# RetNet attention and a soft mixture of experts on one Trainium2 core: the remainder's steps and batch 1's steps in another order, the start's casts and the down weights' layout changed

## The chip, the cores and the metric

The kernel runs on one core of one Trainium2 chip. The metric is the device time of one execution in microseconds. Three runs of the kernel before gave 570.39, 568.17 and 568.40 us; the median is 568.4. One execution was profiled, and every instruction time below comes from it.

## The reference

Two stages, the second on the first one's output. Sizes: batch B = 8, heads H = 8, sequence S = 576, head width D = 64; N = 4608 tokens, model width 512, E = 4 experts, F = 1024.

```python
gamma = 1.0 - 2.0 ** (-5.0 - np.arange(H))
Dmat = np.where(rel >= 0, gamma[:, None, None] ** rel, 0.0)     # rel = i - j
ret = (q @ k.T / sqrt(D)) * Dmat                                # no softmax
x = (ret @ v) as [B * S, H * D]
p = domain_probs / (domain_probs.sum(-1, keepdims=True) + 1e-09)
for e in range(E):
    h = np.maximum(x @ w1[e], 0.0)
    out += p[:, e:e + 1] * (h @ w2[e])
```

Every token passes through all four experts.

## The kernel before, in words

**Attention in chunks.** The decay splits into a factor per query and one per key. Keys are multiplied with theirs when they are cast to bf16 (`cast`, tables `gk`), results with the query's when they leave PSUM (`gq`). What stays is a lower triangle, so the 576 positions of a batch are worked as four chunks of 128 and a remainder of 64 (R). Within a chunk: scores (keys by queries) times a triangle `tri`, then values. From the chunks before: a state, keys transposed by values, summed over the chunks in PSUM (`kvp`) and copied by ScalarE after each chunk to `sbd`, two heads as a block diagonal. Heads go in four pairs (NP = 4).

The methods, with the lines of the profile:

- `cast` (L222, L224; L375 to L379 for batch 0) and `cast_rem` (L227, L230): float32 to bf16, on the engine given.
- `Tc`, `Trem` (L285, L249): transposes of queries and keys by TensorE; `dmaT` (L256): the same by DMA, issued by SP.
- `S` with `Smat` and `Smask` (L264, L271): scores of two head pairs over all chunks, then the masks on VectorE. `Sc` (L297, L301): scores of one chunk for all pairs. `Srem` (L324, L328): scores of the remainder.
- `O` (L338 values, L343 states, L347 product on VectorE into `xT`), `Oc` (L310, L315, L317) and `Orem` (L354, L359, L361): results of two pairs, of one chunk, of the remainder.
- `kv` (L237, L242): state of one chunk.

Batch 0 has a class of its own, `AttP`, which works in four units (two halves of the sequence by two halves of the heads; L389 to L457) as its inputs land. Batch 1 is worked chunk by chunk (`Tc`, `Sc`, `kv`, `Oc`), batches 2 to 7 by head pairs. PSUM has three buffers for the experts (`ps_mm`), four for attention (`ps_at`, in turn) and one for states.

**Experts in tiles of 512 tokens.** `moe(nt)` is a generator for one of nine tiles. For each expert it makes eight blocks of `hT` (four 512-wide matmuls each, `ph`, L468; ScalarE's Relu copies them out, L487), then four blocks of output (eight 512-wide matmuls each, `po`, L497), which ScalarE writes (first expert, L501) or VectorE adds to `acc` (L503). After each block it yields, so a tile has 48 groups. Matrices are named by their tiles: up `wt_267`, `wt_496`, `wt_500`, `wt_504` for experts 0 to 3, down `wt_491`, `wt_498`, `wt_502`, `wt_506`.

**What sets the order.** Every engine works through its own queue in program order, and the program is written out by hand: `plan` maps a group's number to the attention steps put behind that group. TensorE meets the attention of batch nt + 1 between the matmuls of tile nt. For batches 2 to 7:

```python
            at(19 if nt == 1 else 17, lambda: state["A"].S([0, 1]))
            at(24, lambda: state["A"].O([0, 1]))
            at(27, lambda: state["A"].S([2, 3]))
            at(32, lambda: state["A"].O([2, 3]))
            at(37, lambda: state["A"].Srem())
            at(40, lambda: state["A"].Orem())
```

Batch 1 goes into groups 40 to 47 of tile 0: `Tc(c)` at 40, 42, 44, 46, `Sc(c)` and `kv(c)` one group later, `Oc(c)` another group later. The last chunk's scores and results stand between the tiles, around the first three half blocks of tile 1 (`lead`).

**The start.** SP issues the loads of batch 0 in twelve parts (L85). GpSimd casts keys and values of each unit and, for the second unit, queries; ScalarE casts the other units' queries (L377). GpSimd also issues the loads of weights, which convert float32 to bf16 on the way: the first up matrix in two halves (L119), behind key casts of the third and fourth unit, then the first down matrix (`load_w2`, L124) and the other six. The first matmul of the experts is at 19.43 us.

A down matrix is loaded with two neighbouring rows for each partition; row pairs mean that hidden unit 2p + i of a block of 256 stands in partition p, so `up` takes every second column of the up matrix (L467).

Of the kernel before, what the change touches and what calls it, by code (L numbers as in the profile page):

```python
# [9 lines left out]
FP32 = mybir.dt.float32  # L10
# [4 lines left out]
MULT = mybir.AluOpType.mult  # L15
# [5 lines left out]
def kernel(  # L21
# [10 lines left out]
    nc = tc.nc  # L32
    B, H, S, D = q.shape
# [6 lines left out]
    R = S - NCH * C  # L40
    SM = NCH * C
    NP = H // 2
# [7 lines left out]
    allp = list(range(NP))  # L50
# [9 lines left out]
    ps_at = ctx.enter_context(tc.tile_pool(name="ps_at", bufs=4, space=PSUM))  # L60
# [12 lines left out]
    state = {}  # L73
# [39 lines left out]
    w1_sb, w2_sb = [], []  # L113
# [7 lines left out]
    def load_w2(e):  # L121
        wt2 = wpool.tile([128, NFC, Dm], BF16, tag=f"w2_{e}", name="wt2")
        w2_sb.append(wt2)
        return nc.gpsimd.dma_start(out=wt2[:, :, :].rearrange("p (fo fi) d -> p fo (fi d)", fi=2),  # L124
                                   in_=moe_w2[e].rearrange("(fo p fi) d -> p fo (fi d)", p=128, fi=2))


    load_paired(0)
# [49 lines left out]
    gq = const.tile([128, NP, S], FP32)  # L178
# [7 lines left out]
    sbd = const.tile([128, NCH, NP, 128], BF16)  # L186
# [15 lines left out]
    xT = const.tile([128, NDC, N], BF16)  # L202
# [5 lines left out]
    class Att:  # L208
# [120 lines left out]
                    st[:, j], s[j], tri[:R, :R].unsqueeze(1).to_broadcast([R, NP, R]), op=MULT)  # L329
            self.sT["r"] = st  # L330

        def O(self, pairs):
            b = self.b
            os = [ps_at.tile([128, SM], FP32, tag="at", name="o") for _ in pairs]
            for p, o in zip(pairs, os):
                for c in range(NCH):
                    for j in range(2):
                        nc.tensor.matmul(o[64 * j:64 * j + 64, c * C:(c + 1) * C],  # L338
                                         lhsT=self.m["v"][:, c, 2 * p + j, :], rhs=self.sT[p][:, j, c, :],
                                         start=(c == 0), stop=False, skip_group_check=True)  # L340
            for p, o in zip(pairs, os):
                for c in range(1, NCH):
                    nc.tensor.matmul(o[:, c * C:(c + 1) * C], lhsT=sbd[:, c - 1, p, :],  # L343
                                     rhs=self.qkT[:, 0, p, c * C:(c + 1) * C],
                                     start=False, stop=(c == NCH - 1), skip_group_check=True)
            for p, o in zip(pairs, os):
                nc.vector.tensor_tensor(xT[:, p, b * S:b * S + SM], o, gq[:, p, 0:SM], op=MULT)  # L347

        def Orem(self):
            b = self.b  # L350
            o = ps_at.tile([128, NP, R], FP32, tag="at", name="orem")
            for p in range(NP):
                for j in range(2):
                    nc.tensor.matmul(o[64 * j:64 * j + 64, p, :],  # L354
                                     lhsT=self.r["v"][:, 2 * p + j, :], rhs=self.sT["r"][:, j, p, :],
                                     start=(p == 0), stop=False, skip_group_check=True)
            for n in self.rem_states:
                for p in range(NP):
                    nc.tensor.matmul(o[:, p, :], lhsT=sbd[:, n, p, :], rhs=self.qkT[:, 0, p, SM:S],  # L359
                                     start=False, stop=(p == NP - 1), skip_group_check=True)  # L360
            nc.vector.tensor_tensor(xT[:, :, b * S + SM:(b + 1) * S], o, gq[:, :, SM:S], op=MULT)  # L361

# [96 lines left out]
    def moe(nt, lead=0):  # L461
        n0 = nt * NT

        def up(ph, e, fc, ts):
            for dc in range(NDC):

                w = w1_sb[e][:, dc, (fc // 2) * 256:(fc // 2 + 1) * 256].rearrange("p (f i) -> p f i", i=2)  # L467
                nc.tensor.matmul(ph[:, ts], lhsT=w[:, :, fc % 2],  # L468
                                 rhs=xT[:, dc, n0 + ts.start:n0 + ts.stop], start=(dc == 0), stop=(dc == NDC - 1))

        acc = [apool.tile([128, Dm], FP32, tag="acc", name="acc") for _ in range(NSUB)]
        for e in range(E):
            hT = hpool.tile([128, NFC, NT], BF16, tag="hT")
            for fc in range(NFC):
                if e == 0 and fc < lead:
                    if fc == 0:
                        early = [ps_mm.tile([128, NT], FP32, tag="mm", name="ph") for _ in range(lead)]
                        for x in range(lead):
                            up(early[x], e, x, slice(0, NT // 2))
                            if x != 1:  # L480
                                yield
                    ph = early[fc]
                    up(ph, e, fc, slice(NT // 2, NT))
                else:
                    ph = ps_mm.tile([128, NT], FP32, tag="mm", name="ph")
                    up(ph, e, fc, slice(0, NT))
                nc.scalar.activation(hT[:, fc, :], ph, Relu)  # L487
                yield
            for ns in range(NSUB):
                t = nt * NSUB + ns  # L490
                pe = probs[:, e, t:t + 1]
                last = t == NTT - 1 and e == E - 1
                w = Dm // 2 if last else Dm
                for d in range(0, Dm, w):
                    po = ps_mm.tile([128, w], FP32, tag="mm", name="po")
                    for fc in range(NFC):
                        nc.tensor.matmul(po, lhsT=hT[:, fc, ns * 128:(ns + 1) * 128],  # L497
                                         rhs=w2_sb[e][:, fc, d:d + w], start=(fc == 0), stop=(fc == NFC - 1))
                    a = acc[ns][:, d:d + w]
                    if e == 0:  # L500
                        nc.scalar.activation(a, po, Copy, scale=pe)  # L501
                    else:
                        nc.vector.scalar_tensor_tensor(a, po, pe, a, op0=MULT, op1=ADD)  # L503
                    if e == E - 1:
                        eng = nc.scalar if last and d // w % 2 else nc.sync
                        eng.dma_start(out=out[n0 + ns * 128:n0 + (ns + 1) * 128, d:d + w], in_=a)
                yield


    a0 = AttP(0)  # L510
# [7 lines left out]
    for x, (hf, u) in enumerate(UNITS):  # L518
        a0.T(hf, u, nc.scalar)
        if x < 2:  # L520
            load_gq((2 + x,))
        if x == 0:
            warm(4)
        else:
            a0.O(*UNITS[x - 1])
        if x < 3:
            a0.cast("k", *UNITS[x + 1], nc.gpsimd)
            if x:
                load_w1(0, x - 1)
            a0.cast("q", *UNITS[x + 1], nc.scalar if x else nc.gpsimd)  # L530
            a0.cast("v", *UNITS[x + 1], nc.gpsimd)
        a0.S(hf, u)
        if x == 0:
            warm(2)
        a0.kv(hf, u)
# [14 lines left out]
    for nt in range(n_nt):  # L550
        plan = {}

        def at(g, *fs):
            plan.setdefault(g, []).extend(fs)

        if nt == 0:
# [17 lines left out]
            for c, g in enumerate((40, 42, 44, 46)):  # L574
                at(g, lambda c=c: state["a1"].Tc(c))
                if c < 3:
                    at(g + 1, lambda c=c: state["a1"].Sc(c), lambda c=c: state["a1"].kv(c, allp))
                    at(g + 2, lambda c=c: state["a1"].Oc(c))
            at(47, lambda: state["a1"].kv(3, allp))
        elif nt + 1 < B:  # L580
            if nt == 1:
                a1 = state["a1"]
                at(0, lambda: a1.cast_rem(nc.gpsimd))
                at(2, a1.Trem)
                at(4, a1.Srem)
                at(6, a1.Orem)
            def begin(b=nt + 1):
                A = state["A"] = Att(b)
                for c in range(NCH):
                    for n in "kqv":  # L590
                        A.cast(n, c, nc.gpsimd)
                A.cast_rem(nc.gpsimd)
                for c in range(NCH + 1):
                    A.dmaT(c)
                if b + 1 < B:
                    load(b + 1)

            at(7 if nt == 1 else 0, begin)
            for n, g in zip(range(NCH), (13, 15, 17, 18) if nt == 1 else (9, 11, 13, 15)):
                at(g, lambda n=n: state["A"].kv(n, allp))  # L600
            at(19 if nt == 1 else 17, lambda: state["A"].S([0, 1]))
            at(24, lambda: state["A"].O([0, 1]))
            at(27, lambda: state["A"].S([2, 3]))
            at(32, lambda: state["A"].O([2, 3]))
            at(37, lambda: state["A"].Srem())
            at(40, lambda: state["A"].Orem())
        for g, _ in enumerate(tiles[nt]):
            for f in plan.get(g, ()):
                f()
# [35 lines left out]
```

## Time and profile before

| what | value |
|---|---|
| three runs | 570.39, 568.17, 568.40 us; median 568.4 |
| the profiled execution | 570.39 us |
| its span, first to last instruction | 568.6 us, 8301 instructions |
| TensorE matmuls busy | 555.3 us, 98% |
| TensorE weight loads busy | 264.9 us, 47% |
| VectorE, ScalarE, GpSimd busy | 159.1, 228.9, 95.1 us |
| mean granted clock of TensorE | 0.993 |
| one steady tile, from one expert block to the same one of the next tile (213.28 to 273.58 us) | 60.3 us |

Matmuls are pipelined, and each is listed with its whole length, so the starts tell more than the busy time: a 512-wide matmul is listed with 379 ns, but 32 of them start within 6.91 us. "PEld" is TensorE's weight load; "64*128" in a matmul's row are the rows and columns of the array that it uses, and "64x128 bf16" its moving operand. A timeline row gives start, length, engine, line, operation, tiles and how many instructions it merges.

### The profile page before, as it was taken

Reading aid. Unit: us, or ns where it says so; the run is one execution under the profiler, and the core shown is the slowest. Engines: PE = TensorE matmul, PEld = TensorE weight load, DVE = VectorE, ACT = ScalarE, POOL = GpSimd, SP = SyncE. Lnnn points to the kernel's source line nnn. Section 1 sums busy time; section 2 is a strip of 40 time slices with the busy share of each in tenths; the row PEclk is TensorE's granted clock in tenths of the full one; section 3 lists DMA queues with packets and bytes.
Section 4 is the critical chain, followed back from the end, with each engine's and each line's share of the span. In section 5 each row is a group of like instructions: output and inputs, shape, how many; then the busy total and the mean of one; then the engine's idle time right before and its main releaser. Section 6 shows DMA issues by size and latency. Waiting matters only on the chain.

```text
span 568.6 us, 8301 instructions
## 1 busy us (share of the span) xinstructions
PE 555.3 (98%) x3418; PEld 264.9 (47%) x3418; DVE 159.1 (28%) x267; ACT 228.9 (40%) x409; POOL 95.1 (17%) x141
## 2 busy tenths in 40 slices
PE   7699999999999999999999999999999999999997
PEld 4444455444444444444444444444444444444443
DVE  5203254054204420342124320542044202220222
ACT  6252354622363235533463236223632353335332
POOL 7400437015001420114010601050000000000000
PEclk9799999999999999999999999999999999999999
DMA  9999997493259015940577037802300100010002
GB/s 234 202 206 205 207 196 175 84 206 46 83 93 221 11 39 115 194 63 1 134 159 115 1 111 140 159 1 84 74 2 1 50 25 1 0 66 10 1 0 75
DMA packets 146102, 53.84 MB, mean 95 GB/s; under 512 B 130540, under 2 KB 137964, under 8 KB 146064
## 3 DMA queue, kind: packets, MB, share of 16 engines
q1 hardware_dynamic: 141168, 44.79, 37.8%
q0 software_dynamic: 4752, 8.39, 8.0%
q8 instruction: 27, 0.44, 0.3%
q10 hardware_dynamic: 144, 0.13, 0.1%
q14 instruction: 11, 0.09, 0.1%
HBM read 45.16 MB, written 9.44 MB: 96 GB/s over the span
## 4 chain that ended last, share of the span: by engine, by line
PE 95%; DMA 2%; SPq 1%; DVE 0%; issue 0%; ACT 0%; POOL 0%
PE ph L468 44%; PE po L497 44%; DMA wt_267<-in_moe_w_dram 1%; PE o L338 1%; PE kvp L237 1%; SPq L85 1%; DMA raw_k<-in_k_dram 1%; PE o L343 1%; PE orem L354 0%; PE orem L359 0%; PE ptc L285 0%; PE oc L310 0%; PE oc L315 0%; POOL km L375 0%; ACT sbd L242 0%
## 5 line engine op out<-in xcount | busy, mean ns | idle before, releaser
L487 ACT ACTIVATE hT<-ph 128x512 bf16<-128x512 f32 x288 | 171.7, 597 | 279.3 <-PE ph L468 277.8
L497 PEld LDWEIGHTS <-hT 128*128 128x128 bf16 x1160 | 112.5, 98 | 131.4
L503 DVE SCALAR_TENSOR_TENSOR acc<-po,probs,acc 128x512 f32<-128x512 f32 (+1 forms) x109 | 81.3, 746 | 225.9 <-PE po L497 219.0
L468 PE MATMUL ph<-xT,wt_267 128*128 128x512 bf16 (+1 forms) x312 | 66.9, 372 | 5.5 <-DMA wt_267<-in_moe_w_dram 4.7
L468 PE MATMUL ph<-xT,wt_496 128*128 128x512 bf16 x288 | 66.8, 379 | 0.0
L468 PE MATMUL ph<-xT,wt_504 128*128 128x512 bf16 x288 | 66.2, 379 | 0.0
L468 PE MATMUL ph<-xT,wt_500 128*128 128x512 bf16 x288 | 65.8, 379 | 0.0
L497 PE MATMUL po<-wt_502,hT 128*128 128x512 bf16 x288 | 64.6, 379 | 0.0
L497 PE MATMUL po<-wt_491,hT 128*128 128x512 bf16 x288 | 64.4, 379 | 0.0
L497 PE MATMUL po<-wt_506,hT 128*128 128x512 bf16 (+1 forms) x296 | 64.1, 373 | 0.0
L497 PE MATMUL po<-wt_498,hT 128*128 128x512 bf16 x288 | 64.0, 379 | 0.0
L222 POOL TENSOR_TENSOR km<-raw_k,gk 128x512 bf16<-128x512 f32 x28 | 29.2, 1042 | 148.2 <-PE kvp L237 81.8
L468 PEld LDWEIGHTS <-wt_267 128*128 128x128 bf16 x312 | 30.9, 101 | 37.6 <-DMA wt_267<-in_moe_w_dram 5.1
L468 PEld LDWEIGHTS <-wt_500 128*128 128x128 bf16 x288 | 27.4, 98 | 31.5
L468 PEld LDWEIGHTS <-wt_504 128*128 128x128 bf16 x288 | 27.2, 98 | 30.7
L468 PEld LDWEIGHTS <-wt_496 128*128 128x128 bf16 x288 | 27.0, 98 | 28.8
L501 ACT ACTIVATE acc<-po,probs 128x512 f32<-128x512 f32 x36 | 24.7, 687 | 36.1 <-PE po L497 36.1
L224 POOL CAST vm<-raw_v 128x512 bf16<-128x512 f32 x28 | 17.2, 614 | 96.1 <-PE o L338 93.6
L242 ACT ACTIVATE sbd<-kvp 64x256 bf16<-64x256 f32 x56 | 20.9, 372 | 3.7 <-PE kvp L237 3.1
L224 POOL CAST qm<-raw_q 128x512 bf16<-128x512 f32 x28 | 17.1, 609 | 2.8 <-DMA raw_q<-in_q_dram 1.0
L347 DVE TENSOR_TENSOR xT<-o,gq 128x512 bf16<-128x512 f32 x24 | 15.4, 685 | 5.9 <-PE o L343 5.4
L237 PEld LDWEIGHTS <-km 128*128 128x128 bf16 x112 | 8.3, 98 | 6.8 <-issue 0.8
(251 smaller groups left out, 235.6 us busy)
## 6 DMA issues: line engine op xcount, KB each, us to landing
out_dram<-acc SPq DMA_DIRECT2D x35, 256.0 KB, 2.0
raw_k<-in_k_dram SPq DMA_DIRECT2D x32, 256.0 KB, 5.1
raw_q<-in_q_dram SPq DMA_DIRECT2D x32, 256.0 KB, 5.0
raw_v<-in_v_dram SPq DMA_DIRECT2D x32, 256.0 KB, 5.1
wt_267<-in_moe_w_dram POOLq DMA_DIRECT2D x2, 512.0 KB, 8.1
wt_491<-in_moe_w_dram POOLq DMA_DIRECT2D x1, 1024.0 KB, 11.6
wt_496<-in_moe_w_dram POOLq DMA_DIRECT2D x1, 1024.0 KB, 15.3
wt_498<-in_moe_w_dram POOLq DMA_DIRECT2D x1, 1024.0 KB, 20.3
```

The source lines that it names most:

```text
L85: nc.sync.dma_start(out=pairs_of(state[b][n, hf])[:, h], in_=src[b, h, 256 * hf:256 * hf + 256, :].rearrange("h (p j) d -> p h (j d)", j=2))
L222: eng.tensor_tensor(o, i, gk[:, c, :].unsqueeze(2).to_broadcast([128, H, D]), op=MULT)
L224: eng.tensor_copy(o, i)
L237: nc.tensor.matmul(self.kvp[:, p, :], lhsT=flat(self.m["k"][:, n, h, :]), rhs=flat(self.m["v"][:, n, h, :]), start=(n == 0 and i == 0), st ...
L242: nc.scalar.activation(sbd[j:j + 64, n, a:z, j:j + 64], self.kvp[j:j + 64, a:z, j:j + 64], Copy)
L338: nc.tensor.matmul(o[64 * j:64 * j + 64, c * C:(c + 1) * C], lhsT=self.m["v"][:, c, 2 * p + j, :], rhs=self.sT[p][:, j, c, :], start=(c == ...
L347: nc.vector.tensor_tensor(xT[:, p, b * S:b * S + SM], o, gq[:, p, 0:SM], op=MULT)
L468: nc.tensor.matmul(ph[:, ts], lhsT=w[:, :, fc % 2], rhs=xT[:, dc, n0 + ts.start:n0 + ts.stop], start=(dc == 0), stop=(dc == NDC - 1))
L487: nc.scalar.activation(hT[:, fc, :], ph, Relu)
L497: nc.tensor.matmul(po, lhsT=hT[:, fc, ns * 128:(ns + 1) * 128], rhs=w2_sb[e][:, fc, d:d + w], start=(fc == 0), stop=(fc == NFC - 1))
L501: nc.scalar.activation(a, po, Copy, scale=pe)
L503: nc.vector.scalar_tensor_tensor(a, po, pe, a, op0=MULT, op1=ADD)
```

## The change

Five edits:

1. `load_w2` loads row by row: for each partition eight rows of 512 instead of four pairs of rows; `up` takes 128 neighbouring columns. The matrix is the same size.
2. `O` can take the remainder with it (`rem=True`): its values (L354 before) come behind the pairs' values, its states (L359) behind the pairs' states, its product behind theirs. `Orem` alone is now `O` with no pairs.
3. Batches 2 to 7: `Srem` stands at group 24, ahead of `O([0, 1])`, and the remainder's results are made in `O([2, 3], rem=True)` at group 32. Groups 37 and 40 hold nothing more.
4. Batch 1: `kv(c)` ahead of `Sc(c)`, and `Oc(c)` one chunk later, behind `Sc(c + 1)` in the same group (behind `Tc(3)` by a group for chunk 2).
5. The start: the queries of the third and fourth unit are cast by GpSimd, ahead of the issue of each half of the first up matrix.

```diff
@@ load_w2
-        return nc.gpsimd.dma_start(out=wt2[:, :, :].rearrange("p (fo fi) d -> p fo (fi d)", fi=2),
-                                   in_=moe_w2[e].rearrange("(fo p fi) d -> p fo (fi d)", p=128, fi=2))
+        return nc.gpsimd.dma_start(out=wt2, in_=moe_w2[e].rearrange("(fc p) d -> p fc d", p=128))
@@ O
-        def O(self, pairs):
+        def O(self, pairs, rem=False):
             os = [ps_at.tile([128, SM], FP32, tag="at", name="o") for _ in pairs]
+            orem = ps_at.tile([128, NP, R], FP32, tag="at", name="orem") if rem else None
             for p, o in zip(pairs, os):
...
+            if rem:
+                for p in range(NP):
+                    for j in range(2):
+                        nc.tensor.matmul(orem[64 * j:64 * j + 64, p, :],
+                                         lhsT=self.r["v"][:, 2 * p + j, :], rhs=self.sT["r"][:, j, p, :],
+                                         start=(p == 0), stop=False, skip_group_check=True)
             for p, o in zip(pairs, os):
...
+            if rem:
+                for n in self.rem_states:
+                    for p in range(NP):
+                        nc.tensor.matmul(orem[:, p, :], lhsT=sbd[:, n, p, :], rhs=self.qkT[:, 0, p, SM:S],
+                                         start=False, stop=(p == NP - 1), skip_group_check=True)
             for p, o in zip(pairs, os):
                 nc.vector.tensor_tensor(xT[:, p, b * S:b * S + SM], o, gq[:, p, 0:SM], op=MULT)
+            if rem:
+                nc.vector.tensor_tensor(xT[:, :, b * S + SM:(b + 1) * S], orem, gq[:, :, SM:S], op=MULT)
         def Orem(self):
...
+            Att.O(self, [], rem=True)
@@ up
-                w = w1_sb[e][:, dc, (fc // 2) * 256:(fc // 2 + 1) * 256].rearrange("p (f i) -> p f i", i=2)
-                nc.tensor.matmul(ph[:, ts], lhsT=w[:, :, fc % 2],
+                nc.tensor.matmul(ph[:, ts], lhsT=w1_sb[e][:, dc, fc * 128:(fc + 1) * 128],
@@ start
             a0.cast("k", *UNITS[x + 1], nc.gpsimd)
+            a0.cast("q", *UNITS[x + 1], nc.gpsimd)
             if x:
                 load_w1(0, x - 1)
-            a0.cast("q", *UNITS[x + 1], nc.scalar if x else nc.gpsimd)
             a0.cast("v", *UNITS[x + 1], nc.gpsimd)
@@ batch 1
                 if c < 3:
-                    at(g + 1, lambda c=c: state["a1"].Sc(c), lambda c=c: state["a1"].kv(c, allp))
-                    at(g + 2, lambda c=c: state["a1"].Oc(c))
+                    at(g + 1, lambda c=c: state["a1"].kv(c, allp), lambda c=c: state["a1"].Sc(c))
+                if c > 0:
+                    at(g + 1, lambda c=c: state["a1"].Oc(c - 1))
@@ batches 2 to 7
-            at(24, lambda: state["A"].O([0, 1]))
+            at(24, lambda: state["A"].Srem(), lambda: state["A"].O([0, 1]))
             at(27, lambda: state["A"].S([2, 3]))
-            at(32, lambda: state["A"].O([2, 3]))
-            at(37, lambda: state["A"].Srem())
-            at(40, lambda: state["A"].Orem())
+            at(32, lambda: state["A"].O([2, 3], rem=True))
```

More of the change, by code (lines that the diff above doesn't have):

```diff
@@ L345, in O @@
                                      start=False, stop=(c == NCH - 1), skip_group_check=True)
+            if rem:
[3 more added lines that the diff above has]
+                                         start=False, stop=(p == NP - 1), skip_group_check=True)
             for p, o in zip(pairs, os):
                 nc.vector.tensor_tensor(xT[:, p, b * S:b * S + SM], o, gq[:, p, 0:SM], op=MULT)
+            if rem:
+                nc.vector.tensor_tensor(xT[:, :, b * S + SM:(b + 1) * S], orem, gq[:, :, SM:S], op=MULT)
         def Orem(self):
[L350 to L361, printed above, removed]
+            Att.O(self, [], rem=True)
     class AttP(Att):
```

## The prediction

> **What bounds the kernel now.** I read the page first, part 4, the chain that ended last:
>
> ```profile
> PE 95%; DMA 2%; SPq 1%; DVE 0%; issue 0%; ACT 0%; POOL 0%
> ```
>
> TensorE is the chain, so a change counts where it alters what TensorE streams, or where TensorE still waits. For the waits I took the chain in order of time:
>
> ```profile
> 7.38 5.42 DMA raw_k<-in_k_dram
> ...
> 12.88 0.99 POOL km L375
> 13.87 8.06 DMA wt_267<-in_moe_w_dram
> ...
> 39.90 6.91 PE ph L468 x32
> ```
>
> The one long wait is at the start: the last key cast on GpSimd, the second half of the first up matrix issued behind it (L119), landed at 21.93 us, and only then the first experts. From there on the chain is TensorE. The last line gives its pitch: 6.91 / 32 = 0.216 us for a 512-wide matmul, and it is the same for L468 (up, weights read with a step of two columns) as for L497 (down, weights without a step). So the change's plain columns in L468 are worth nothing: no load of weights shows in that pitch.
>
> Then the timeline of TensorE in one steady tile, around the remainder's two blocks:
>
> ```profile
> 258.79 1.89 PE L468 MATMUL ph<-xT,wt_504 128*128 128x512 bf16 x8
> 260.61 0.21 PE L324 MATMUL sr_2841<-qkT 64*64 64x64 bf16 x1
> ...
> 260.73 0.19 PE L324 MATMUL sr_2842<-qkT 64*64 64x64 bf16 x1
> 260.85 2.77 PE L468 MATMUL ph<-xT,wt_504 128*128 128x512 bf16 x12
> 263.55 0.31 PE L354 MATMUL orem<-sTr,vrb 64*64 64x64 bf16 x8
> 263.79 0.29 PE L359 MATMUL orem<-qkT,sbd 128*128 128x64 bf16 x4
> 263.92 0.81 PE L468 MATMUL ph<-xT,wt_504 128*128 128x512 bf16 x3
> ```
>
> Read starts against pitch. Eight matmuls from 258.79 are streamed at 260.52; the scores start at 260.61: 0.09 lost. The last scores start at 260.73 and need about 0.03; L468 starts at 260.85: 0.09 again. Twelve from there end at 263.44, the values start at 263.55: 0.1. Eight values take about 0.15 and L359 starts 0.24 after them: 0.09. From L359 to L468, both 128*128, four matmuls of about 0.03 fill the 0.13: nothing lost. So TensorE loses 0.09 us wherever the rows*columns of the array change, and none where they stay. The two blocks put 0.33 and 0.48 us into the stream, four junctions of 0.09 among it.
>
> **The change part by part, batches 2 to 7.** Nothing is added or removed on TensorE; the order moves. Before: block L338, L343 has two junctions (in, and 128*64 to 128*128), Srem two, Orem two. After: L468, Srem, L338, L343, L468 has in, 64*64 to 128*64, 128*64 to 128*128: three where there were four. And L468, L338, L354, L343, L359, L468 has in, 128*64 to 64*64, 64*64 to 128*128: three where there were four. Two junctions saved per batch, 0.19 us, in six batches 1.1 us. The kind 64*64 to 128*64 is not in the trace. The nearest is inside L410, where 64 rows become 128 with the columns kept: eight matmuls start from 7.52, the fourth at about 7.69, the fifth at about 7.86, so it costs 0.09 too. I take 0.09; bounds: at nothing, the gain would be four junctions per batch, 2.2 us; at double, none, 0.
>
> What hides the rest: Srem needs the remainder's transposes, issued by SP at 111.78 in the tightest tile and landing in about 2.4 us, while the new place is at 122.3; its masks (0.42 us each on VectorE) come ahead of two 0.69 us products, and the next scores, which need those PSUM buffers, start 2.7 us after that block: 2 x 0.42 + 2 x 0.6 is under that. Were that cover gone, the excess would be a stall of tenths. The joint block's third PSUM buffer, orem, is one whose mask ended about 3 us before. The remainder's tiles come free some 10 us earlier (263.9 to 253.6), so GpSimd's last cast, which waits until 263.99, moves up; SP's transposes behind it stay, as they follow the output stores until 274.8.
>
> **Batch 1 in tile 0.**
>
> ```profile
> 75.49 0.68 DVE L301 TENSOR_TENSOR sT<-s_948,tri 128x512 bf16<-128x512 f32 x1
> 75.98 0.63 PE L310 MATMUL oc<-sT,vm 128*64 128x128 bf16 x8
> 80.34 0.41 PE L310 MATMUL oc<-sT,vm 128*64 128x128 bf16 x8
> ```
>
> The first values start at 75.98 while the second mask runs until 76.17; they span 0.63 against 0.41 for the next ones: a stall of 0.22, which goes, as the values of a chunk now follow the next chunk's scores. Two groups (kv, scores, values) have one junction fewer: 0.19. Sum 0.4. What is late next: at the tile's end the product of chunk 2 (0.69 on VectorE) now stands ahead of chunk 3's masks, but its matmuls (0.66) move down by as much, so the stall of 0.8 us before the second halves of L468 at 92.03 stays. The buffer that each Oc takes was freed by a copy one group earlier.
>
> **Down weights.** The rows halve from 4 KB to 2 KB of source, so packets double. The trace has both sizes in the software queue, DMA view of 14.5 to 18.5 us (first up matrix, loaded in halves with rows of this size) and of 22 to 30 us (long rows):
>
> ```profile
> q0 software_dynamic: 722, 0.72, 118.1%
> ```
>
> ```profile
> q0 software_dynamic: 878, 1.74, 111.2%
> ```
>
> That is 0.72 / 4 = 0.180 MB/us against 1.74 / 8 = 0.217: a down matrix (1 MB) takes 5.8 us instead of 4.8. From 31 us on the queue alternates packet for packet with the raw loads (921 to 922 between 40 and 50 us); worked out from 105 and 162 ns a packet, a down matrix then takes about 7.5 instead of 5.6. Landings before and first uses: 26.8 for 32.8, 37.7 for 46.6, 49.2 for 61.8, 60.7 for 78.5. Lateness grows to 1, 3, 5 and 7 us, under each margin of 6, 9, 12.6 and 17.8. Cost nothing; if GpSimd needs twice its 0.75 us to issue each, nothing still, since its next work is at 38 us. The remainder load that waits for the first down matrix starts 1 to 2 us later and is needed at 48.5 where it landed at 43.7.
>
> **Start.** Two query casts go from ScalarE to GpSimd, 0.67 us each by the pitch of L379 (8.65 to 9.33), each ahead of a half of the first up matrix. First half issued at 11.85 instead of 11.18, second at 15.2 instead of 13.87. TensorE's transposes of unit 3 start some 0.65 later, inside the wait that ends at 21.93. What of 1.34 reaches the landing? Nothing, if the queue sets it: from 14 us on all engines are full and the halves follow each other. All, if it lands 8.06 after its issue as before. Between 12.9 and 14 us the queue moved 51 packets, 0.28 us of its rate, and these are lost for certain. I take 0.5, nearer to the full queue; bounds 0 and 1.34.
>
> **Sum.** 1.1 + 0.4 - 0.5 = 1.0 us less. The profiled execution took 570.39 (span 568.6 and 1.8 around it), so 569.4; it was the slowest of three, the others 568.17 and 568.40. On the median 568.4 the same sum gives 567.4.
>
> **Rivals.** First, *the start eats it* (0.14): the full 1.34, and the clock with it.
>
> ```profile
> 20.00:22.00 2.00, 0.03 (x1) 0.03 (x2) 0.00 (x0) 0.00 (x0) 1.11 (x2) 0.74 1.13 212
> 22.00:24.00 2.00, 2.00 (x26) 1.36 (x27) 0.27 (x1) 0.00 (x0) 0.00 (x0) 0.50 1.12 213
> ...
> 26.00:28.00 2.00, 2.00 (x12) 1.30 (x9) 0.00 (x0) 1.03 (x2) 0.00 (x0) 0.55 1.11 209
> 28.00:30.00 2.00, 2.00 (x13) 1.11 (x13) 1.58 (x5) 1.19 (x3) 0.00 (x0) 1.00 1.12 210
> ```
>
> These are windows; the third number from the end is the granted clock. It was half from about 21 to 27.8 us. If half speed lasts half as long again as these 6.8 us, 3.4 more, that is 1.7 us of work: 568.4 - 1.5 + 1.34 + 1.7 = 569.9, still within 0.5%.
>
> Second, *slower*: down loads become bound by packets (0.06). If a short packet cost the 162 ns of a long one, each down matrix would take 11 us, the second would land near 49 for 46.6, the third and fourth some 2 and 0.5 late on top: 4.8 us of stalls, 568.4 - 1.0 + 4.8 = 572.2. It decides once a down matrix takes over 10 us. Against it: the halves of the first up matrix landed 2.5 us apart.
>
> Third, *no gain from order* (0.10): junctions cost the same however they are ordered; then only the stall of 0.22 goes, 568.4 - 0.2 + 0.5 = 568.7. The Trainium skill's "TensorE: Matmul & The Clock Gate", Part 2, says that weight loads are pulled ahead of running matmuls into a background buffer; by that rule a junction would cost nothing and none could be saved. The trace disagrees: 0.09 us at each.
>
> Fourth, *the clock stays up* (0.08): TensorE's last attention work ends about 0.65 later, so the idle stretch before 21.97 shrinks; if the clock isn't halved, 5.8 us at half speed become 2.9: 568.4 - 1.0 - 2.9 = 564.5. The same page, Part 1, says that the clock falls after an idle window of about 3.4 us and that windows run free of the kernel; by that rule a gap cut from 5.0 us to somewhat less would seldom escape. The trace agrees in that the half-speed stretch is about two such windows long.
>
> **How the numbers follow.** Forecast 0.62, its own range 566 to 568.4. With no gain from order and most of the start rival, and the runs of before spreading over 2.2 us, 565.6 to 570.0 holds 8 in 10. About 0.5% (2.8 us) is what a measurement here can tell from no change: faster by more 0.08 (the clock), slower by more 0.07 (packets and a rest), the same 0.85.
>
> **What would show it.** Right: blocks of Srem with L338 and of L338 with L354 putting 0.19 us less into a tile's stream; no 0.63 at the first values of batch 1; steady tiles 60.1 us apart instead of 60.3; no wait of L497 for a down matrix. Wrong: the first L468 after 23 us, a wait for a down matrix, or a clock at half past 28 us.

## The result, and the profile after

The changed kernel takes 563.19 us (median of six runs, 562.65 to 563.85) against 568.63 for the kernel before (six runs, 568.17 to 570.39): ratio 0.990, 95% interval 0.9885 to 0.9914. That is 5.4 us less where 1.0 was forecast, and outside the range given. The profiled execution took 563.04 us with a span of 561.2; against the profiled one of before that is 7.4 us of span.

The chain that ended last, in order of time. Columns are start, length, what:

```profile
16.06 11.17 DMA wt_491<-in_moe_w_dram
...
27.28 7.08 PE po L497 x32
```

The wait for the second half of the first up matrix is gone from the chain. In its place stands the first down matrix (`wt_491`), on which the first `po` waits at 27.28. In the kernel before that matmul started at 32.83. The start thus gave 5.55 of the 7.4 us.

TensorE's timeline shows how. First the kernel before, rows that the prediction did not show:

```profile
19.43 0.28 PE L468 MATMUL ph<-xT,wt_267 128*128 128x256 bf16 x1 [2.46 <-DMA wt_267<-in_moe_w_dram]
21.97 0.82 PE L468 MATMUL ph<-xT,wt_267 128*128 128x256 bf16 x3 [2.26 <-DMA wt_267<-in_moe_w_dram]
...
32.83 3.40 PE L497 MATMUL po<-wt_491,hT 128*128 128x512 bf16 x15
```

Then the changed kernel:

```profile
17.92 0.61 PE L468 MATMUL ph<-xT,wt_268 128*128 128x256 bf16 x4 [0.69 <-DMA wt_268<-in_moe_w_dram]
18.46 0.42 PE L446 MATMUL o<-sT,vm 64*64 64x128 bf16 x16
...
27.28 1.04 PE L497 MATMUL po<-wt_491,hT 128*128 128x512 bf16 x4 [0.76 <-DMA wt_491<-in_moe_w_dram]
```

The four matmuls of the first half block were split before: one, a wait of 2.26 us on another load of the same matrix, then three. Now they run together. Yet all four read columns of the first half of the matrix alone. The built program of before (its instructions as the framework wrote them out, each with the semaphores it waits for) says what the second one waited for:

```
L468 Ldweights wt_267 [waits DMASW0_49]
L468 Matmult ph<-xT,wt_267 128x256
L468 Ldweights wt_267 [waits DMASW1_49]
```

DMASW0 is counted up by the load of the first half, DMASW1 by that of the second. In the changed program the first block has only the first of the two waits. With the step of two columns, the dependency tracking that writes the waits took a reading of the first half for one of the second. With plain columns it does not. In a partition the second half's load writes four separate pieces, from element 512 to element 4095. The weight load without the false wait starts at element 0, ahead of them all; the one with it starts at element 1024, between the first piece and the last. So the tracking may compare outer bounds only when a read has a step; that reason is an inference.

The clock followed. These are windows; the third number from the end is the granted clock:

```profile
20.00:22.00 2.00, 2.00 (x18) 1.63 (x17) 0.30 (x1) 1.08 (x2) 2.00 (x4) 1.00 1.04 141
22.00:24.00 2.00, 2.00 (x12) 0.93 (x11) 1.28 (x5) 1.23 (x3) 0.56 (x1) 1.00 1.12 172
```

It was 0.74 and 0.50 before. A steady tile of the changed kernel shows the new order:

```profile
235.82 1.03 PE L468 MATMUL ph<-xT,wt_500 128*128 128x512 bf16 x4
236.78 0.21 PE L323 MATMUL sr_2668<-qkT 64*64 64x64 bf16 x1
...
236.90 0.19 PE L323 MATMUL sr_2669<-qkT 64*64 64x64 bf16 x1
237.02 0.64 PE L338 MATMUL o<-sT,vm 128*64 128x128 bf16 x16
237.59 0.51 PE L349 MATMUL o<-qkT,sbd 128*128 128x128 bf16 x6
237.94 2.75 PE L468 MATMUL ph<-xT,wt_500 128*128 128x512 bf16 x12
...
246.46 0.64 PE L338 MATMUL o<-sT,vm 128*64 128x128 bf16 x16
247.03 0.31 PE L344 MATMUL orem<-sTr,vrb 64*64 64x64 bf16 x8
247.27 0.51 PE L349 MATMUL o<-qkT,sbd 128*128 128x128 bf16 x6
247.62 0.28 PE L355 MATMUL orem<-qkT,sbd 128*128 128x64 bf16 x4
247.73 0.60 PE L497 MATMUL po<-wt_502,hT 128*128 128x512 bf16 x2
```

Start to start, a last pair of scores at 236.90 and the values at 237.02: about 0.03 for the pair and 0.09 lost, so the kind 64*64 to 128*64 costs what the others do. The tile's two joint blocks put 1.25 and 1.37 us into the stream (start of the next expert matmul less the pitch), where the four blocks of before put 1.01, 1.01, 0.34 and 0.46: 0.20 less per tile. Between the same expert matmuls of two neighbouring tiles it is 0.22 (60.08 us apart instead of 60.30).

### The profile page after: what moved, and what is told of

Read it like the earlier page. It is cut to its first block, busy times and chain, and to the rows that moved or that the text cites. A ratio compares the mean times of both kernels' runs of the same rounds, so it can differ in the third digit from the quotient of the medians.

```text
span 561.2 us, 8302 instructions
## 1 busy us (share of the span) xinstructions
PE 552.4 (98%) x3418; PEld 265.4 (47%) x3418; DVE 158.3 (28%) x267; ACT 227.6 (41%) x407; POOL 96.6 (17%) x143
## 4 chain that ended last, share of the span: by engine, by line
PE 94%; DMA 3%; POOL 1%; SPq 1%; DVE 0%; ACT 0%; issue 0%
PE po L497 44%; PE ph L468 43%; DMA wt_491<-in_moe_w_dram 2%; PE o L338 1%; PE kvp L236 1%; DMA raw_k<-in_k_dram 1%; PE o L349 1%; SPq L85 1%; POOL km L377 0%; PE orem L344 0%; PE ptc L284 0%; POOL wt_268 L119 0%; PE oc L309 0%; PE orem L355 0%; POOL vm L381 0%; POOL qm L381 0%
## 5 line engine op out<-in xcount | busy, mean ns | idle before, releaser
L497 PEld LDWEIGHTS <-hT 128*128 128x128 bf16 x1160 | 112.4, 98 | 132.4 <-DMA wt_491<-in_moe_w_dram 1.2
L468 PE MATMUL ph<-xT,wt_496 128*128 128x512 bf16 x288 | 66.8, 379 | 0.0
L468 PE MATMUL ph<-xT,wt_268 128*128 128x512 bf16 (+1 forms) x312 | 64.7, 363 | 1.5 <-DVE xT L316 0.8
L468 PE MATMUL ph<-xT,wt_500 128*128 128x512 bf16 x288 | 65.8, 379 | 0.0
L497 PE MATMUL po<-wt_491,hT 128*128 128x512 bf16 x288 | 64.5, 379 | 0.8 <-DMA wt_491<-in_moe_w_dram 0.8
L497 PE MATMUL po<-wt_502,hT 128*128 128x512 bf16 x288 | 64.6, 379 | 0.0
L497 PE MATMUL po<-wt_506,hT 128*128 128x512 bf16 (+1 forms) x296 | 64.1, 373 | 0.0
L468 PE MATMUL ph<-xT,wt_504 128*128 128x512 bf16 x288 | 64.1, 379 | 0.0
L497 PE MATMUL po<-wt_498,hT 128*128 128x512 bf16 x288 | 64.0, 379 | 0.0
L468 PEld LDWEIGHTS <-wt_268 128*128 128x128 bf16 x312 | 30.0, 98 | 32.6 <-issue 0.9
L468 PEld LDWEIGHTS <-wt_504 128*128 128x128 bf16 x288 | 28.0, 98 | 33.4
L468 PEld LDWEIGHTS <-wt_500 128*128 128x128 bf16 x288 | 27.3, 98 | 31.6
L468 PEld LDWEIGHTS <-wt_496 128*128 128x128 bf16 x288 | 27.0, 98 | 28.8
```

Of the source, the lines that this page charges most:

```text
L468: nc.tensor.matmul(ph[:, ts], lhsT=w1_sb[e][:, dc, fc * 128:(fc + 1) * 128], rhs=xT[:, dc, n0 + ts.start:n0 + ts.stop], start=(dc == 0), s ...
```

## The experiments

Every time is set against runs of the kernel before on the same chip in the same job.

**Each part alone.** The first four kernels take the change apart. `e1_casts` is edit 5 on the kernel before, `e2_down` edit 1, `e3_order` edits 2 to 4, `e4_pairs` the whole change without edit 1.

```diff
 e1_casts: kernel before, and
+            a0.cast("q", *UNITS[x + 1], nc.gpsimd)
             if x:
                 load_w1(0, x - 1)
-            a0.cast("q", *UNITS[x + 1], nc.scalar if x else nc.gpsimd)
 e2_down: kernel before, and
...
-                                   in_=moe_w2[e].rearrange("(fo p fi) d -> p fo (fi d)", p=128, fi=2))
+        return nc.gpsimd.dma_start(out=wt2, in_=moe_w2[e].rearrange("(fc p) d -> p fc d", p=128))
...
-                nc.tensor.matmul(ph[:, ts], lhsT=w[:, :, fc % 2],
+                nc.tensor.matmul(ph[:, ts], lhsT=w1_sb[e][:, dc, fc * 128:(fc + 1) * 128],
 e3_order: changed kernel, with the lines of e1_casts and e2_down as before
 e4_pairs: changed kernel, with the lines of e2_down as before
```

> The kernel before with the start's query casts alone changed (two casts from ScalarE to GpSimd, each ahead of a half of the first up matrix). Three theories for the 5.4 us that the whole change gained, of which the order of steps (batches 1 to 7) explains about 1.5. T1, issue: the halves of the first up matrix, issued 0.5 and 0.8 us later, no longer land late. Before, one sixteenth of each half landed 2.2 us behind the other fifteen; then here the first expert matmuls start near 18 us instead of 19.4 to 22, the clock stays full, and the time is 564.5 to 565.5. T2, layout: the down weights' short rows do it; then this run stays within 0.7 us of the kernel before, or is slower by up to that. T3, chance of an execution: runs of the same kernel differ by 2 to 4 us whichever edit is made, and the runs of before in this job show both starts.

> The kernel before with the down weights loaded row by row (and the up weights' columns plain) alone. T1, issue of the up halves: no gain at the start, the first down matrix lands 1 us later but under its margin: 568.6 within 0.5. T2, layout: first expert matmuls near 18 us, full clock: 564.5 to 565.5. T3: either, run by run.

> The kernel before with the order of steps alone changed (remainder of batches 2 to 7, batch 1). All theories: steady tiles 60.09 us apart instead of 60.28 (two junctions of 0.09 less), batch 1 about 0.4 shorter, in all 1.5 us less than before, so 566.5 to 567.3, if the start is as before. T3 would also allow a start that differs by 2 to 4 us.

> The whole change without the down weights' part (two rows per part are kept). T1: the start as in the changed kernel, and the wait of 0.9 us for the first down matrix gone, since it takes 4.8 instead of 5.8 us to move: 562.0 to 562.8, faster than both kernels. T2: the start falls back, 566.5 to 567.3. T3: between, by chance.

The kernel before took 568.79 us here (13 runs).

| kernel | median us | ratio, 95% interval |
|---|---|---|
| e1_casts | 568.05 | 0.9993, 0.9977 to 1.001 |
| e2_down | 563.70 | 0.990, 0.988 to 0.992 |
| e3_order | 566.02 | 0.9938, 0.9917 to 0.9959 |
| e4_pairs | 566.89 | 0.9953, 0.9934 to 0.9972 |

The first theory, that the later issue of the halves mattered, fell: the casts alone do nothing that can be told from nothing. The start's gain sits in edit 1, alone and in the whole. Chance as a cause fell too: all runs of `e2_down` were between 563.0 and 564.3, all of `e3_order` between 565.4 and 566.2. But edit 1 has two halves, short rows in the load and plain columns in `up`, and the text of the expectation blamed the rows.

Two of the ranges were missed. `e2_down` is 0.8 us under its range, and alone it has the ratio of the whole change, 0.990, though it lacks the order's gain; in the profiled executions its first `po` came 0.5 us sooner (26.80 against 27.28). `e3_order` is 0.5 under. Its gain of 2.8 us is more than the order's: all four of its runs had a granted clock of 0.996, as with a halved clock of 3.4 us at the start, while six of the 13 runs of before had 0.990 to 0.994. Against the other seven (median 567.69) `e3_order` is 1.7 us faster.

In `e1_casts` the split is still there, 18.12 and 20.66 for the first and second matmul; in `e2_down` four start from 17.20. This and the list of waits gave the next theory: not the rows but the wait on the second half.

**The wait by itself.** `e5_split` takes it away without touching a row or a column: the halves become two tiles, so that a read of one cannot wait for the other. `e6_wait` puts it back into the whole change.

```diff
 e5_split: kernel before, and
+            w1_sb.append(wpool.tile([128, NDC, F], BF16, tag=f"w1_{e}", name="wt1") if part is None else [
+                wpool.tile([128, NDC, F // 2], BF16, tag=f"w1_{e}_{u}", name=f"wt1_{u}") for u in range(2)])
...
+                w, x = (w1_sb[e][fc // 4], fc % 4) if e == 0 else (w1_sb[e], fc)
 e6_wait: changed kernel, and
...
+                if nt == 0 and e == 0 and fc == 0 and dc == 1 and ts.start == 0:
+                    after(mm, second)
...
+                second = load_w1(0, x - 1)
```

> The kernel before, with the two halves of the first up matrix kept as two tiles and nothing else changed (row pairs and the step of two columns stay). Theory W, from the waits written into both programs: in the kernel before the second weight load of the first expert block waits for the second half of the matrix, though it reads the first half alone, because it reads with a step of two columns; in the changed kernel, with plain columns, it waits for the first half only. Then here four half blocks start together near 17.5 to 19 us, the clock stays full, and the time is 562.5 to 563.5, as the down loads stay long and the first of them lands about 1 us before it does with short rows. Rival D, short rows of the down loads themselves help the start: nothing changes here, 568.0 to 569.3.

> The whole change, with the wait for the second half of the first up matrix put back at the second expert matmul. Theory W: the start is that of the kernel before again, first matmul near 18, the next three behind the second half near 20.5 to 22, half a clock for one or two stretches of 3.4 us: 566.0 to 567.3, the order's gain alone. Rival D: 563.2 as with the change.

The kernel before took 567.73 (19 runs). `e6_wait` took 566.13 (ratio 0.9973, 0.9959 to 0.9988). The changed kernel did not run in this job; against its 563.2 in two others the one wait takes back 2.9 us, and by the ratios to before (0.990 and 0.9914) 3.4 to 4.1. The split is there again in its timeline:

```profile
17.30 0.28 PE L468 MATMUL ph<-xT,wt 128*128 128x256 bf16 x1 [0.31 <-DMA wt<-in_moe_w_dram]
20.57 0.82 PE L468 MATMUL ph<-xT,wt 128*128 128x256 bf16 x3 [2.99 <-DMA wt<-in_moe_w_dram]
```

`e5_split` took 565.05 (ratio 0.9953, 0.9936 to 0.9970). The start came as expected, four matmuls from 17.97 and the first `po` at 26.41, with a full clock in every run. The time did not: it is 1.5 us above the range. Its timeline has a wait that neither kernel has, at batch 0's remainder (group 20 of tile 0):

```profile
41.74 0.38 PE L503 MATMUL po<-wt,hT 128*128 128x512 bf16 x1
43.15 0.29 PE L254 MATMUL ptr<-ident,qrb 64*128 64x64 bf16 x4 [1.03 <-POOL qrb L235]
```

The wait is 1.1 us of the miss. The rest may lie in the start of the profiled execution of before, which was a late one: its first `po` was at 32.83, those of `e1_casts`, `e3_order` and `e4_pairs`, with the same false wait, at 30.30 to 30.36. From 30.3 to 26.41, less 1.1, would be a gain of 2.8, an estimate; measured were 2.7.

At the remainder TensorE is over 6 us earlier than in the kernel before, and the remainder's queries, cast at 43.76 there, only 1.3. GpSimd's rows in `e5_split`, then in `e2_down`:

```profile
42.48 0.60 POOL L235 CAST qrb<-raw_qr 64x512 bf16<-64x512 f32 x1 [4.75 <-DMA raw_qr<-in_q_dram]
```

```profile
39.00 0.60 POOL L229 CAST qrb<-raw_qr 64x512 bf16<-64x512 f32 x1 [3.11 <-DMA raw_qr<-in_q_dram]
```

So the short rows do have a part, a later one: with them the remainder's queries land 3.5 us sooner. The queues suggest why. From 33 to 38 us, in the kernel before and in the changed one (packets, MB, share of 16 engines):

```profile
q0 software_dynamic: 461, 0.91, 95.9%
q1 hardware_dynamic: 459, 0.11, 17.3%
```

```profile
q0 software_dynamic: 758, 0.79, 92.5%
q1 hardware_dynamic: 756, 0.19, 29.0%
```

The two queues take turns, packet for packet. With the weights' packets half as large, the raw loads move 0.19 MB instead of 0.11 in the same 5 us, in packets of their own of about the same size (0.25 KB). `e10_mixed` below tests this. The Trainium skill's "DMA: Bandwidth & Descriptors", section "Queues, rings and completion order", has the rule: each engine goes round the queues with work, one packet at a time. The trace agrees, 758 to 756.

**The two terms of the start.** `e8_warm` leaves the wait and fills the time before the first expert block with 20 idle matmuls.

```diff
 e8_warm: kernel before, and
+    warm(20)
     next(tile0)
```

> The kernel before with 20 idle matmuls of TensorE (4.3 us, on zeros, as the start has already) ahead of the first expert block, nothing else changed; the wait for the second half stays. It parts the start's gain into its two terms. If the halved clock is worth 1.7 to 2.9 us of it, and the waiting time itself the rest, 566.0 to 567.0 with a full clock. If the clock is a small part, 568.0 or more.

It took 566.73 (ratio 0.9977, 0.9963 to 0.9991), with a full clock in all ten runs. From its second expert matmul, at 21.03, to its first `po`, at 29.35, are 8.32 us; the kernel before took 32.83 - 21.97 = 10.86 for the same, with the clock halved for 6.8 us. The difference, 2.5 us, is what the halved clock cost in that execution. In `e6_wait`, halved for 6.8 us too, the same stretch takes 10.86; in `e1_casts` and `e3_order`, halved for 3.4 us, 9.64 and 9.91, so there it cost 1.3 to 1.6. The median gained less, 1.0 us, also because the idle matmuls ran on until 20.92, while the last part of the second half had landed at 19.90.

**The order on a start without the wait.** `e7_best` puts edits 2 to 4 on `e5_split`.

> The new order of steps (batches 1 to 7) on the kernel before, with the first up matrix's halves as two tiles; row pairs, long rows and the start's casts as before. Theory W: the start's gain, the order's gain and no wait of 0.9 us for the first down matrix: 561.0 to 562.2, faster than both kernels. Rival D: 566.0, as the order alone.

It took 563.00 (ratio 0.9918, 0.9901 to 0.9934), 0.8 above its range, and its timeline has the same new wait as `e5_split`: the remainder's transposes wait 0.99 us by the profile (1.15 start to start). Long rows spare the wait for the first down matrix and bring this one; the two nearly cancel, and the kernel is level with the changed one.

**Both waits gone.** Two ways: the remainder two to four groups later (`e9_later`), or long rows for the first down matrix and short ones for the others (`e10_mixed`); the changed kernel beside them.

```diff
 e9_later: e7_best, and
-            at(20, a0.Trem)
-            at(22, a0.Srem)
-            at(24, a0.Orem)
+            at(22, a0.Trem)
+            at(24, a0.Srem)
+            at(28, a0.Orem)
...
-            at(25, begin1)
+            at(29, begin1)
 e10_mixed: e7_best, and
+        if e:
+            return nc.gpsimd.dma_start(out=wt2, in_=moe_w2[e].rearrange("(fc p) d -> p fc d", p=128))
...
+                else:
+                    w = w1_sb[e][:, dc, fc * 128:(fc + 1) * 128]
```

> The version with the new order, the first up matrix in two tiles and long rows, which took 563.0 though it has no wait for the first down matrix, and with batch 0's remainder put later: transposes at group 22, scores at 24, results at 28 (20, 22, 24 before), batch 1's casts after that. Theory A, turns of the queue: in that version the transposes wait 1.15 us for the remainder's cast queries, because the raw loads, which take turns packet by packet with the weights, come on more slowly beside long packets. Here that wait is gone: about 1.1 us less, 561.7 to 562.3, faster than the changed kernel. Rival: the wait only moves to the results (values landed at 48.8 there): 562.7 to 563.2.

> The same version with the remainder where it was, and short rows for the down matrices of experts 1 to 3 (long for expert 0 alone). Theory A: the raw loads get more turns while the second down matrix is moved, and the remainder's queries are cast near 40 instead of 42 us: no wait of the transposes, and none of the first down matrix either: 561.7 to 562.3. Rival, row lengths don't matter to the raw loads: 562.7 to 563.3 with the wait of 1.1 us still there.

> The changed kernel once more, beside the two others on the same chip: 562.7 to 563.7, with the wait of 0.9 us for the first down matrix in its profile.

| kernel | median us | all runs | ratio to before (568.30), 95% interval |
|---|---|---|---|
| e9_later | 561.95 | 561.57, 561.78, 562.12, 564.36 | 0.9904, 0.9874 to 0.9933 |
| e10_mixed | 561.52 | 560.98 to 561.88 | 0.9889, 0.9864 to 0.9914 |
| e11_changed | 563.10 | 562.29 to 563.62 | 0.9914, 0.9891 to 0.9936 |

The median of `e9_later` is in its range. Its profile does not test the reason: it is of the slowest of the four runs, 564.36, where the first expert matmul came only at 18.63, the clock was halved for 3.4 us, and TensorE was too late to wait for the queries.

`e10_mixed` is the fastest of all, 0.2 under its range: each of its four runs is below each of the changed kernel's in the same job. It has neither wait. Its first `po` is at 25.30, and the remainder's queries are cast at 37.42, 4.6 us sooner than in `e7_best` (42.03), where near 40 was forecast:

```profile
37.42 0.60 POOL L237 CAST qrb<-raw_qr 64x512 bf16<-64x512 f32 x1 [2.74 <-DMA raw_qr<-in_q_dram]
```

## Why the prediction was wrong

**The step that failed: "the change's plain columns in L468 are worth nothing".** I priced them by the pitch of the matmuls, and that price was right: 0.216 us before and after. But the columns had a second price, in the waits. The chain showed 8.06 us of load `wt_267` ending where the first experts began, and I read it as data that those matmuls needed. Two rows spoke against it. The first L468 ran at 19.43 alone, before that load had landed (the text ahead of the prediction says so too), and the list of waits put L468 down with two on `wt_267`, 4.7 us together, the longest 2.5:

```profile
PE ph L468 <- DMA wt_267<-in_moe_w_dram: 4.7, 2, 2.5
```

A matrix in two halves, a first block that reads one, and two waits in it: the second was a false one. The two built programs show the difference line by line, and need no run. Put back by itself, the wait cost 2.9 to 4.1 us (`e6_wait`).

From that step the start's gain follows, in the profiled executions: the second expert matmul from 21.97 to 18.04, 3.9 us; the clock, 2.5; the new wait for the first down matrix, 0.9 the other way. That makes 5.5, as measured from start to first `po`. The medians differ by less than the profiled executions, since that execution of before had 6.8 us of half clock and a second half landing at 21.93; in `e1_casts` and `e3_order`, with the same wait, the second matmul came at 20.66 and 20.45, the halved clock lasted 3.4 and the first `po` came at 30.30 and 30.36.

**"The clock stays up"** was a rival with 0.08. It happened, but not as told there: the idle stretch was not shortened by later attention work but by experts that started at once.

**Down weights, "cost nothing".** The step that failed here is the margin. The lateness of the first matrix was about right: with long rows and the same early start (`e7_best`) the first `po` stands 0.2 us behind the block ahead of it, in the changed kernel 0.9 (1.4 in `e11_changed`), where 1 us was forecast. The later matrices landed 1.3, 2.3 and 3.5 us later than before, half of the 3, 5 and 7 forecast. The margin of 6 was gone: it hung on the start, which moved 5.5 us. The prediction's own sign of being wrong, a wait of L497 for a down matrix, came true. One of its rates is a little off, too: the row with 878 packets is of 21.7 to 30 us, so 1.74 MB took 8.3 us and not 8, which is 0.210 MB/us and 5.0 us a matrix instead of 0.217 and 4.8. The worth of short rows for the raw loads was noted (7.5 instead of 5.6 us a matrix) but not followed to its other side, raw loads that come sooner.

**Start, 0.5 us lost.** The start gained, but through edit 1; what the casts did by themselves stays open. `e1_casts` lies between 0.23% faster and 0.1% slower. The second half of the first up matrix was issued at 14.71, 0.8 us later than before, where 15.2 was forecast. The first expert matmul came at 17.92 with the changed casts and at 17.20 without (`e2_down`), but the other kernels with the old casts and no false wait began anywhere from 16.86 (`e10_mixed`) to 18.63 (`e9_later`), so one execution of each can't tell.

**Order, 1.1 + 0.4 us.** Right in mechanism, a little small. From the first `po` to the last the kernel before takes 531.91 us, the changed one 530.12: 1.79. Counted between the same expert matmuls of both, six batches give 0.22 each, 1.30, and batch 1 gives 0.49; its first values no longer stall:

```profile
72.30 0.41 PE L309 MATMUL oc<-sT,vm 128*64 128x128 bf16 x8
```

Steady tiles are 60.08 us apart (remainder's scores at 236.78 and 296.86), where 60.1 was forecast. The rival without a gain from order fell.

## What to carry to other kernels

When a load ends a wait, ask whether the waiting instruction reads what that load brings, and compare the waits of both built programs before pricing an edit by its instructions; a change of addressing can add or remove a wait. A margin holds only as long as the start before it does: after a change that moves the start, look at every wait that was hidden by it. Transfers in two queues share by packets, so the shape of one sets the pace of the other.

## What the runs showed of the hardware

Every change of the array's rows and columns between blocks of bf16 matmuls on 64 or 128 rows and columns cost 0.09 us, in all the kinds met here, also from 64*64 to 128*64 and back. Blocks with the same rows and columns followed each other at no loss: four matmuls of 0.03 us fill the 0.11 from L355 at 247.62 to L497 at 247.73.

The halved clock came in stretches of 3.4 and 6.8 us; a stretch of 6.8 cost 2.5 us, more than all edits of the order (1.8). "TensorE: Matmul & The Clock Gate" in the Trainium skill, Part 1, gives windows of about 3.4 us; the stretches agree. Every run without the false wait but one (`e9_later`'s of 564.36, with 0.996) had a granted clock of 0.999 or more; with it, and nothing to fill the time, it was 0.990 to 0.997 in all but one.

Issuing a load of 1 MB in rows twice as many took GpSimd 0.88 to 0.93 us instead of 0.74 to 0.79: twice the packets, a fifth more time.

A load counts its semaphore up in sixteen parts, and one part can land well behind the others. In the profiled execution of before the last part of the second half of the first up matrix came at 21.92, 2.0 us behind the fifteenth (19.96); in `e1_casts` it came 0.6 behind (20.61), in the changed kernel 0.1 (20.42). Why one part lags, and why most in that execution, stays open; the experiments removed the wait for it, not its cause.
